# The third row tile's load moved ahead of a weight load, a copy-out shared by two engines, and four column-tiled sums put into one group

## The chip, the cores and the metric

The kernel runs on one core of a Trainium2 chip. The metric is device time in microseconds (us) of that core; a kernel's time is the median of its runs. A profile is one execution with every instruction recorded; its span, from the first to the last instruction, is some 1.7 us shorter than the time reported for the same execution (196.0 for 197.67 us before the change).

Engine names in the profile are PE (TensorE, matrix products), PEld (its weight loads), DVE (VectorE), ACT (ScalarE), POOL (GpSimd) and SP (SyncE, which issues most transfers).

## The reference, cut to what matters

The input x has 2048 rows of 512 bf16 numbers. Its layer norm feeds two branches: attention with 32 heads of 16 columns over a dilated window of 8 earlier positions, and a gated feed-forward layer 1376 wide. Both are added to x.

```python
xn = _layernorm(x, axis=-1)                       # 2048 x 512
# branch A: H = 32 heads, Dh = 16, window W = 8, dilation 2
qkv = x @ wqkv                                    # wqkv 512 x 1536: Wq, Wk, Wv
logits = einsum("bhsd,bhswd->bhsw", q, kg) * scale
attn = softmax(where(mask, logits, -1e9))
o = einsum("bhsw,bhswd->bhsd", attn, vg)          # the weighted values
# branch B
h = _gelu(xn @ w_gate) * (xn @ w_up)              # 512 x 1376 each
return x + o @ wo + h @ w_down
```

## The kernel before

The rows are worked in four blocks of 512, each of four row tiles of 128 rows. For a row tile, VectorE computes statistics, subtracts the mean and multiplies by the reciprocal of the square root; the tile is transposed, and TensorE projects it to Q, K and V and to the gate and up parts of the feed-forward layer.

The program is not written in the order in which it runs. Python code describes tasks, each with an engine, an estimated duration, what it reads and writes, and a priority; a list scheduler then fixes the order of each engine's instructions and assigns the PSUM banks. A table `SHIFT` moves the priorities of whole groups of tasks and was found by search. So a change of one part can reorder everything else.

Three places are touched by the change. First, the loads at the start. A lower number is issued earlier:

```python
# weights, 512 KB each: Wq, Wk, Wv
t_w = G.task("sp", "ld_w" + nm, 0, mk(), wr=[(I_wq, nm)],
             prio=(-958, -957.5, -898)[i], nbytes=512 * 1024)
...
if p == 0:                       # row tiles 0 and 1, 128 KB each
    for t2 in range(2):
        ...
        t_x = G.task("sp", "ld_x0_%d" % t2, 0, mk_ld(), wr=[(it_x, t2)], prio=-960 + t2,
                     nbytes=128 * 1024)
else:                            # later tiles in pairs, 256 KB
    ...
    t_x = G.task("sp", "ld_x%d" % p, 0, mk_ld(), wr=[(it_x, 0), (it_x, 1)],
                 prio=(0, -957, -897.5, -897)[p] if p < 4 else -950 + p * 20, nbytes=256 * 1024)
```

So the queue carries tile 0, tile 1, Wq, Wk, then tiles 2 and 3 together.

Second, the layer norm and the transposes of block 0. TensorE transposes a tile (four 128x128 pieces into PSUM, the memory that takes TensorE's results) and ScalarE copies all four out at once. The square roots of tiles 0 and 1 run on ScalarE (`NSQA` = 2), those of tiles 2 and 3 on GpSimd. The order of the start is fixed by chains:

```python
t_ev = G.task("act", "evx" + nm, d_act(512 * n), mk_ev(), rd=[it_tp], ...)   # one copy, 512 columns
...
chain(["bnst0", "bnag0", "sub0", "rstd0", "norm0", "bnst1", "bnag1", "sub1", "rstd1", "norm1",
       "bnst2", "bnag2", "ve2", "sub2", "bnst3", "rstd2", "norm2", "bnag3", "ve3", "sub3", "rstd3",
       "norm3", "bnst4"])
...
chain(warm_tasks[:WARM[0]] + ["tpx0_0"] + warm_tasks[WARM[0]:] +
      ["mmt0_0", "tpx0_1", "mmt1_0", "mmt0_1", "tpx1_0", "mmt1_1", "tpx1_1",
       "mmt0_2", "mmt1_2", "mmt0_3", "mmt1_3"])
```

Here `tpx0_0` to `tpx1_1` are the transposes of tiles 0 to 3, and `mmtW_T` is the projection of tile T to Q (W = 0) or K (W = 1). `warm` tasks are matrix products of zeros that run before any data is there.

Third, the sum of the weighted values. VectorE multiplies values by softmax weights into eight buffers a block; TensorE sums over partitions with a 128x32 matrix of ones, in four column tiles (`tile_position`), two of the four sums of a block in a group:

```python
pvr_grp.append((dq, it_pv, it_o))
if len(pvr_grp) == PVR_MERGE:                    # 2
    ...
    for (dq_, itp, it) in grp:
        for half in range(2):
            for d4 in range(4):
                ins = e.matmul(PS[32 * d4:32 * d4 + 32, 512 * it.slot:512 * it.slot + 512],
                               lhsT=E4[:, :], rhs=UNI[:, itp[half].slot, d4, :],
                               start=(half == 0), stop=(half == 1),
                               tile_position=(0, 32 * d4))
    ...
    # then one ScalarE copy (evo) for each sum of the group, PSUM -> OT
```

## Time and profile before

| | kernel before |
|---|---|
| time, median of 4 runs | 197.88 us (197.62 to 197.93) |
| span of the profiled run | 196.0 us |
| fourth row tile's transposes start | 12.15 us |
| last matrix product ends | 193.56 us |
| between the two ("the rest") | 181.41 us |

The busy shares, the waits of TensorE and the chain of waits are shown in the prediction below. These lines of the timeline of the kernel before give start in us, duration in us, engine, line, operation, output<-input, shape and count; in brackets stands the idle time just before, and what ended it.

```profile
6.39 1.07 PE L1076 MATMUL PS<-xnT,Wqkv 128*128 128x128 bf16 x16 [0.26 <-ACT xnT L1037]
...
7.51 1.95 PE L1076 MATMUL PS<-xnT,Wqkv 128*128 128x128 bf16 x32
...
8.13 0.69 DVE L945 BATCH_NORM_STATS2 st<-XIN 128x6 f32<-128x512 bf16 x1 [1.04 <-DMA XIN<-in_A_x_dram]
...
12.15 0.40 PE L1026 MATMUL PS<-ident,XIN 128*128 128x128 bf16 x4 [0.26 <-DVE XIN L1001]
```

The first projections (Q of tile 0) wait for ScalarE's copy. The next ones, at 7.51, are the first that need Wk, and they do not wait: Wk was there by then. The statistics of tile 2 wait 1.04 us for a transfer, because its load stands behind Wk.

### The profile page before, as it was taken

Reading aid. Unit: us, or ns where it says so; the run is one execution under the profiler, and the core shown is the slowest. Engines: PE = TensorE matmul, PEld = TensorE weight load, DVE = VectorE, ACT = ScalarE, POOL = GpSimd, SP = SyncE. Lnnn points to the kernel's source line nnn. Section 1 sums busy time; section 2 is a strip of 40 time slices with the busy share of each in tenths; the row PEclk is TensorE's granted clock in tenths of the full one; section 3 lists DMA queues with packets and bytes.
Section 4 is the critical chain, followed back from the end, with each engine's and each line's share of the span. In section 5 each row is a group of like instructions: output and inputs, shape, how many; then the busy total and the mean of one; then the engine's idle time right before and its main releaser. Section 6 shows DMA issues by size and latency. Waiting matters only on the chain.

```text
span 196.0 us, 3243 instructions
## 1 busy us (share of the span) xinstructions
PE 190.6 (97%) x1223; PEld 91.1 (46%) x1223; DVE 153.8 (79%) x241; ACT 104.0 (53%) x169; POOL 9.6 (5%) x33
## 2 busy tenths in 40 slices
PE   7879999999999999999999999999999999999995
PEld 2675444444444344444444444443444444344484
DVE  5689997999699899989989984999966638962232
ACT  3467674777976649502647801667739500776000
POOL 6021000101000000000001100000000000000000
PEclk9999999999999999999999999999999999999999
DMA  5999998949934452262399346003892250020121
GB/s 137 364 410 274 331 201 138 270 116 229 213 72 108 107 151 68 64 168 93 107 204 222 61 113 183 27 0 110 211 229 43 57 160 29 27 59 0 33 87 40
DMA packets 34783, 27.03 MB, mean 138 GB/s; under 512 B 11248, under 2 KB 33232, under 8 KB 34768
## 3 DMA queue, kind: packets, MB, share of 16 engines
q1 hardware_dynamic: 34768, 26.83, 54.0%
q8 instruction: 9, 0.15, 0.3%
q14 instruction: 6, 0.05, 0.1%
HBM read 19.99 MB, written 5.26 MB: 129 GB/s over the span
## 4 chain that ended last, share of the span: by engine, by line
PE 93%; DMA 3%; DVE 2%; SPq 1%; issue 0%; POOL 0%; DVEq 0%
PE PS L1357 36%; PE PS L1436 19%; PE PS L1120 18%; PE PS L1432 7%; PE PS L1326 4%; PE PS L1204 4%; DMA XIN<-in_A_x_dram 3%; PE PS L1076 2%; PE PS L1392 2%; PE PS L1197 1%; DVE st L945 1%; SPq L881 0%; SPq L929 0%; DVE XIN L1001 0%; POOL sq L969 0%
## 5 line engine op out<-in xcount | busy, mean ns | idle before, releaser
L1436 PE MATMUL PS<-Wd,HT 128*128 128x512 bf16 (+2 forms) x209 | 41.3, 345 | 0.0
L1357 PE MATMUL PS<-xnT,Wu 128*128 128x512 bf16 x160 | 40.6, 379 | 0.0
L1357 PE MATMUL PS<-xnT,Wg 128*128 128x512 bf16 x160 | 40.3, 379 | 0.0
L1367 ACT ACTIVATE GG<-PS 128x512 bf16<-128x512 f32 x40 | 23.7, 601 | 28.9 <-PE PS L1357 27.7
L1305 DVE TENSOR_TENSOR UNI<-BS,PT 128x2048 bf16<-128x2048 bf16 x32 | 37.1, 1217 | 2.2 <-PE PS L1326 0.8
L1174 DVE TENSOR_TENSOR UNI<-QT,KT 128x2048 bf16<-128x2048 bf16 x32 | 37.4, 1217 | 0.3 <-PE PS L1326 0.3
L1120 PE MATMUL PS<-xnT,Wqkv 128*128 128x512 bf16 x160 | 36.0, 379 | 0.0
L1374 ACT ACTIVATE UU<-PS 128x512 bf16<-128x512 f32 x40 | 24.0, 600 | 10.5 <-PE PS L1357 10.4
L1436 PEld LDWEIGHTS PS<-Wd,HT 128*128 128x128 bf16 x209 | 19.6, 98 | 18.6
L1456 DVE TENSOR_TENSOR OB<-PS,XR 128x512 bf16<-128x512 f32 (+2 forms) x19 | 11.5, 605 | 17.7 <-PE PS L1436 17.7
L1357 PEld LDWEIGHTS PS<-xnT,Wg 128*128 128x128 bf16 x160 | 15.2, 98 | 19.8 <-issue 0.8
L1357 PEld LDWEIGHTS PS<-xnT,Wu 128*128 128x128 bf16 x160 | 15.4, 98 | 19.4 <-ACT GG L1367 0.8
L1120 PEld LDWEIGHTS PS<-xnT,Wqkv 128*128 128x128 bf16 x160 | 15.4, 98 | 19.2 <-ACT KT L1137 0.4
L1379 DVE TENSOR_TENSOR HT<-GG,UU 128x512 bf16<-128x512 bf16 x40 | 16.1, 420 | 8.8 <-ACT UU L1374 8.4
L1144 ACT ACTIVATE VT<-PS 128x512 bf16<-128x512 f32 x16 | 9.6, 598 | 14.4 <-PE PS L1120 14.4
L1432 PE MATMUL PS<-Wo,OT 128*128 128x512 bf16 (+2 forms) x76 | 16.9, 345 | 0.0
L945 DVE BATCH_NORM_STATS2 st<-XIN 128x6 f32<-128x512 bf16 x16 | 10.6, 684 | 2.0 <-DMA XIN<-in_A_x_dram 2.0
L1337 ACT ACTIVATE OT<-PS 128x512 bf16<-128x512 f32 x16 | 8.7, 594 | 5.4 <-PE PS L1326 5.4
L1432 PEld LDWEIGHTS PS<-Wo,OT 128*128 128x128 bf16 x76 | 7.2, 98 | 7.0
L1137 ACT ACTIVATE KT<-PS 128x512 bf16<-128x512 f32 x12 | 7.2, 597 | 4.8 <-PE PS L1120 4.8
L1130 ACT ACTIVATE QT<-PS 128x512 bf16<-128x512 f32 x12 | 7.2, 598 | 3.8 <-PE PS L1120 3.8
L969 POOL TENSOR_TENSOR sq<-ve,mhalf 128x2 bf16<-128x2 f32 (+1 forms) x8 | 5.5, 686 | 64.3 <-DVE ve L956 64.3
(62 smaller groups left out, 134.1 us busy)
## 6 DMA issues: line engine op xcount, KB each, us to landing
BS<-vt_scratch SPq DMA_DIRECT2D x64, 128.5 KB, 3.5
vt_scratch<-VT SPq DMA_DIRECT2D x16, 128.0 KB
XR<-in_A_x_dram SPq DMA_DIRECT2D x16, 128.0 KB, 2.1
XIN<-in_A_x_dram SPq DMA_DIRECT2D x7, 256.0 KB, 5.9
out_dram<-OB SPq DMA_DIRECT2D x14, 128.0 KB, 2.0
Wqkv<-in_A_wqkv_dram SPq DMA_DIRECT2D x3, 512.0 KB, 4.3
Wg<-in_B_w_gate_dram SPq DMA_DIRECT2D x1, 1280.0 KB
Wu<-in_B_w_up_dram SPq DMA_DIRECT2D x1, 1280.0 KB
```

Of the source, the lines that this page charges most:

```text
L945: return lambda e: e.bn_stats(out=st[:, t, :], in_=XIN[:, it.slot, t2, :])
L1120: ins = e.matmul(PS[:, 512 * it.slot:512 * it.slot + HWD], lhsT=lhsT, rhs=xnT[:, itx.slot, kt, c0:c0 + HWD], start=(kt == 0), stop=(kt == 3))
L1144: return lambda e: e.activation(out=VT[:, ito.slot, 0:HWD], in_=PS[:, 512 * it.slot:512 * it.slot + HWD], func=ACTF.Identity)
L1174: return lambda e: e.tensor_tensor(out=UNI[:, it.slot, :, :], in0=bass.AP(QT, (itq.slot * 4 + g) * 512, [[NQT * 4 * 512, 128], [0, 4], [1, ...
L1305: return lambda e: e.tensor_tensor(out=bass.AP(UNI, ito.slot * 2048, [[NUNI * 2048, 128], [512, 4], [128, 4], [1, 128]]), in0=bass.AP(BS, ...
L1357: ins = e.matmul(PS[0:M, 512 * it.slot:512 * it.slot + 512], lhsT=Wx[:, kt, j * 128:j * 128 + M], rhs=xnT[:, itx.slot, kt, :], start=(kt = ...
L1367: return lambda e: e.activation(out=GG[0:M, ito.slot, :], in_=PS[0:M, 512 * it.slot:512 * it.slot + 512], func=ACTF.Gelu_apprx_tanh)
L1374: return lambda e: e.activation(out=UU[0:M, ito.slot, :], in_=PS[0:M, 512 * it.slot:512 * it.slot + 512], func=ACTF.Identity)
L1379: return lambda e: e.tensor_tensor(out=HT[0:M, ito.slot, j, :], in0=GG[0:M, ig.slot, :], in1=UU[0:M, iu.slot, :], op=ALU.mult)
L1432: ins = e.matmul(PS[:, 512 * it.slot:512 * it.slot + CW], lhsT=OT[:, ito.slot, dq, ti * 128:(ti + 1) * 128], rhs=Wo[:, dq, c0:c1], start=( ...
L1436: ins = e.matmul(PS[:, 512 * it.slot:512 * it.slot + CW], lhsT=HT[:, ith.slot, j, ti * 128:(ti + 1) * 128], rhs=Wd[:, j, c0:c1], start=Fal ...
L1456: return lambda e: e.tensor_tensor(out=OB[:, ito.slot, 0:CW], in0=PS[:, 512 * it.slot:512 * it.slot + CW], in1=XR[:, itx.slot, c0:c1], op= ...
```

## The change

It has two aims. At the start, tiles 2 and 3 are loaded apart and tile 2 comes ahead of Wk, so that its layer norm can begin while Wk is still on its way; the first copy-out is split between ScalarE and VectorE; the square roots of tiles 2 and 3 move to ScalarE. Later, all four sums of a block form one column-tiled group, so that TensorE changes its tiling mode less often. `SHIFT` and the scheduler's tolerance were searched anew. The core of the diff, with cuts marked by "...":

```diff
 SHIFT = {
-    "acc0": 47, "acc1": -436, "acc3": 127, ...
+    "acc0": -425, "acc2": -535, "acc3": 96, ...
 }
-             TOL=dict(pe=0.6, act=-0.3, dve=-0.3, pool=-0.3, sp=0.0))
+             TOL=dict(pe=0.6, act=-0.3, dve=0, pool=-0.3, sp=0.0))
...
-    NSQA = cfg.get("NSQA", 2)
+    NSQA = cfg.get("NSQA", 4)
...
-    QUOTAS = cfg.get("QUOTAS", dict(tp=2, qkv=2, lg=2, o=cfg.get("PVR_MERGE", 2), ffn=3,
+    QUOTAS = cfg.get("QUOTAS", dict(tp=2, qkv=2, lg=2, o=cfg.get("PVR_MERGE", 4), ffn=3,
...
-    PVR_MERGE = cfg.get("PVR_MERGE", 2)
+    PVR_MERGE = cfg.get("PVR_MERGE", 4)
...
-        WARM = cfg.get("WARM", (9, 1))
+        WARM = cfg.get("WARM", ([512] * 8 + [128], [512, 128]))
...
-            if p == 0:
+            if p < 2:
                 for t2 in range(2):
...
-                    t_x = G.task("sp", "ld_x0_%d" % t2, 0, mk_ld(), wr=[(it_x, t2)], prio=-960 + t2,
-                                 nbytes=128 * 1024)
+                    t_x = G.task("sp", "ld_x%d_%d" % (p, t2), 0, mk_ld(), wr=[(it_x, t2)],
+                                 prio=((-960, -959), (-957.8, -956.5))[p][t2], nbytes=128 * 1024)
...
+                if p == 0 and grp[0] == 0:
+                    def mk_ev2(it=it_t2, itx=XTI[b], o=o):
+                        return lambda e: e.tensor_copy(
+                            out=xnT[:, itx.slot, 2:4, o:o + 128],
+                            in_=PSB[:, 1024 * it.slot + 256:1024 * it.slot + 512].rearrange("q (k c) -> q k c", k=2))
+                    t_of["evy" + nm] = G.task("dve", "evy" + nm, d_dve(256), mk_ev2(), rd=[it_t2], ...)
+                nk = 2 if "evy" + nm in t_of else 4
...
-        chain(["bnst0", "bnag0", "sub0", "rstd0", "norm0", "bnst1", "bnag1", "sub1", "rstd1", "norm1",
-               "bnst2", "bnag2", "ve2", "sub2", "bnst3", "rstd2", "norm2", "bnag3", "ve3", "sub3", "rstd3",
-               "norm3", "bnst4"])
+        chain(["bnst0", "bnag0", "sub0", "rstd0", "norm0", "bnst1", "bnag1", "evy0_0", "sub1", "rstd1", "norm1",
+               "bnst2", "bnag2", "sub2", "rstd2", "norm2", "bnst3", "bnag3", "sub3", "rstd3", "norm3", "bnst4"])
...
+                chain(["evk0_0", "sq3"])
```

## The prediction

> **What bounds the kernel now.** I read three views of the profile of the kernel before, in this order: the page's busy shares (part 1), the waits of TensorE alone, then the chain that ended last in order of time. Busy shares first, to see which engine could be the bound at all:
>
> ```profile
> PE 190.6 (97%) x1223; PEld 91.1 (46%) x1223; DVE 153.8 (79%) x241; ACT 104.0 (53%) x169; POOL 9.6 (5%) x33
> ```
>
> TensorE is at 97%. A busy share can hide waits, so next all waits of TensorE, longest first (us in total, times, longest):
>
> ```profile
> PE PS L1026 <- DVE XIN L1001: 1.4, 2, 1.1
> PE PS L864 <- DVE wsrc L813: 1.2, 1, 1.2
> PE PS L1076 <- ACT xnT L1037: 0.3, 1, 0.3
> ```
>
> That is the whole list: 2.9 us, and by their lines (transposes L1026, warm-up L864, the first projections L1076) all of it is start-up. The chain (start us, us, what) shows where start-up ends and what follows:
>
> ```profile
> 2.74 5.37 DMA XIN<-in_A_x_dram
> 8.11 0.02 issue
> 8.13 0.70 DVE st L945
> ...
> 10.90 0.61 POOL sq L969
> ...
> 11.74 0.36 DVE XIN L1001
> 12.10 0.05 issue
> 12.15 0.40 PE PS L1026 x4
> 12.55 3.57 PE PS L1076 x64
> ...
> 97.23 1.84 PE PS L1204 x32
> 99.08 0.86 PE PS L1326 x16
> 99.94 5.29 PE PS L1357 x24
> 105.22 0.98 PE PS L1326 x16
> 106.20 1.83 PE PS L1357 x8
> ```
>
> Two things are to be seen. From 12.15 us, where the fourth row tile's transposes start, to 193.56 us the chain is TensorE alone: 181.4 us without a gap. Before that it is the arrival of the third and fourth row tiles (one 256 KB transfer, landed 8.11), then VectorE's layer norm of both, with a square root on GpSimd in the middle. So time can be won in two places only: before 12.15, or in the cost of TensorE's own instructions after it. After 193.56 there are an addition and a store, which the change leaves alone.
>
> **What the Trainium skill says.** TensorEngine Tiling (Array Packing), section Key Properties: "Mode switching requires drain". The trace agrees, and prices it: 16 column-tiled matmuls (L1326) take 0.98 us after ordinary ones but 0.86 right behind another column-tiled group (at 99.08), so 0.12 to enter; the 8 ordinary ones after them take 1.83 against 1.73 for 8 elsewhere in the chain, so 0.10 to leave. TensorE: Matmul & The Clock Gate, section HAM clock gate: the array starts at half clock and is released after about 3.4 us of activity, in a window that does not start with the kernel. The trace agrees: nine 512-wide warm-up matmuls take 4.02 us (0.45 each), later ones 0.216. DMA: Bandwidth & Descriptors, section Queues, rings and completion order: an engine consumes its descriptors in ring order; that is why moving an issue ahead of a 512 KB weight moves its landing. No landing of a single piece in the trace contradicts it. Perfetto Trace Analysis, section Optimizing Scalar/DVE Operations: a fixed cost per operation, so that halves cost more than half. I use it for one estimate below.
>
> **The change, part by part.**
>
> 1. Row tile order. The queue carried tiles 0 and 1 (256 KB), Wq, Wk (512 KB each), tiles 2+3 (256 KB). It will carry tiles 0, 1, Wq, tile 2, Wk, tile 3. By the stretches of the trace the transfers had moved 0.71 MB by 5.0 us, 1.10 by 6.0, 1.46 by 7.0, 1.83 by 8.0. Tiles 2+3 end at 1.57 MB, moved at 7.3, and landed at 8.11: 0.8 later. With the same lag (estimates): Wq, at 0.79 MB, lands about 6.0 in both; tile 2 at 0.92 MB: 5.5 + 0.8 = 6.3 instead of 8.1; Wk at 1.44 MB: 7.7 instead of about 7.4; tile 3 unchanged at 8.1.
>
> 2. First copy-out by two engines, and a shorter warm-up. Eight wide and one quarter-wide warm-up matmuls instead of nine wide end 0.3 us sooner, so the first transposes start when the normalised tile is there (4.79) at about 4.85, not 5.06. ScalarE's copy of 512 columns takes 0.60; I estimate 0.36 for half of it. VectorE's half fits after its second aggregate (ends 5.60) and I estimate 0.35. The first projections then start near 6.0, not 6.39, unless Wq lands later.
>
> 3. Square roots of tiles 2 and 3 on ScalarE, not GpSimd: 0.30 (L959) for 0.15 + 0.61 (L956, L969), and no hand-over through VectorE.
>
> Walk the new start, each duration from the trace of before. VectorE: tile 1 normalised at about 6.9 (7.10 before; its copy delays it 0.35, the earlier square root pays that back). Statistics 0.69, aggregate 0.18, square root 0.30, reciprocal 0.15, scale 0.35 with hand-overs: tile 2 normalised at 8.7. The order of instructions on ScalarE shows one snag: tile 1's copy-out now stands behind tile 2's square root, so it runs 8.1 to 8.7, and tile 1's Q projection can't start before 8.8 (8.4 before). It takes 0.9: 9.7; transposes of tile 2: 9.9; tile 1's K projection: 10.8. Tile 3: statistics from 8.7, after it landed, to 9.35, normalised about 10.4, in time. So the fourth transposes start near 10.8 instead of 12.15: **1.3 us saved**, on the path.
>
> 4. One column-tiled group per block for the weighted sums, not two. Matmuls stay: 128 L1326 instructions. Only mode changes go. Before: 4 groups for the logits and 8 for the sums, one of which (99.08) stands directly behind a logits group, so 11 excursions. After, by the instruction order: 4 + 4, none adjacent, so 8. Three fewer at 0.12 + 0.10: **0.66 us saved**, on the path since TensorE has no slack. Its price: all eight products of a block (8 x 1.217 us of VectorE, L1305) must be ready at once, and four PSUM banks are held until ScalarE has made four copies (4 x 0.594, L1337) where two were held.
>
> 5. New shifts: the order of the rest changes on all engines, with the same work. Nothing is saved where TensorE has no gap; gaps can only be added.
>
> Sum: 1.3 + 0.66 = 2.0 us of 197.85, so 195.9. I add 0.1 for small gaps in a reshuffled order: **196.0 us**, 0.9% less.
>
> **The rivals.**
>
> (a) A new wait in the middle takes the saving back. For it: a merged group waits for the last of eight products, VectorE is at 90% or more in about half of the slices before 160 us, four banks are held for 2.4 us, and every block has been reordered. Against it: the schedule keeps its 1.6 us margin for TensorE behind other engines, which left no wait in the kernel before; and behind each merged group except one the order has three or more matmul groups of 0.86 us, and ScalarE copies at 0.6, so it catches up. A wait of 0.3 us per block would make it 197.2; the whole 2 us would make it "no change".
>
> (b) Start-up gains only the first copy-out, because transfers bind. If tile 2 lands at 7.3 instead of 6.3, statistics start 0.4 later and all behind them: 196.4. If Wk came only at 8.5, tile 1's Q projection would wait behind K of tile 0 and slip by about 0.6: 196.6. Against both: the queue moves 340 to 385 KB per us by then, and the order of bytes is known.
>
> (c) Start-up gains more. If ScalarE's square root did not hold tile 1's copy-out (or were earlier), tile 3's normalisation at 10.4 would be the limit: 0.4 more, 195.6.
>
> (d) The gate weights bind. Wg starts near 18.0 us instead of 18.7. The bytes up to the end of Wg and Wu are moved by about 13 and 16.5 us, so this is hidden anyway; it would show as a TensorE wait on a transfer.
>
> **Range and chances.** Low: rival (c) plus a little, 195.2. High: (a) with a few tenths per block or (b), 197.2. For 2% faster the time would have to be under 193.9; more than 4 us would have to go, and no waits of that size exist: 2.9 us of TensorE waits in all, 1.2 of which come before any data. Faster 2%. For 2% slower rival (a) would need some 6 us of new waits in a schedule made to avoid them: 2%. Same: 96%.
>
> **What would show it right or wrong.** In the chain of the kernel after: the last normalisation-bound transposes near 10.8 (9.9 to 11.3 supports step 3; 12 refutes it); the VectorE statistics of tile 2 start straight behind the normalisation of tile 1 and are no longer released by the transfer. The chain from there on is TensorE alone, some 180.75 us long, ending about 191.6. Merged groups of 32 L1329 matmuls take 1.84 each, four of them. The waits of TensorE list no line beyond start-up; a wait of the merged group on VectorE products, or of a feed-forward group on a ScalarE copy, would be rival (a). The prediction would be wrong most likely through such waits, which I can't see in an instruction order without times.

## The result, and the profile after

| | before | after |
|---|---|---|
| time, median of 4 runs | 197.88 us (197.62 to 197.93) | 196.44 us (196.34 to 196.53) |
| span of the profiled run | 196.0 us | 194.8 us |
| first projections that need Wk start | 7.51 us | 8.30 us |
| fourth row tile's transposes start | 12.15 us | 11.22 us |
| last matrix product ends | 193.56 us | 192.38 us |
| the rest | 181.41 us | 181.16 us |

The ratio of after to before is 0.993, with a 95% interval of 0.9913 to 0.9947: 0.7% less time, well inside 2%. A ratio here is the mean time of one kernel's runs over that of the other's runs of the same rounds, so it is not quite the ratio of the medians quoted beside it. Executions over 1.5% slower than the fastest of the same kernel are left out of the means.

The busy shares of the kernel after (page, part 1) move little; its 1205 matrix instructions are not fewer in the program but missing in the record, since the weight loads beside them count 1224:

```profile
PE 187.7 (96%) x1205; PEld 91.3 (47%) x1224; DVE 153.3 (79%) x240; ACT 101.5 (52%) x171; POOL 16.0 (8%) x31
```

The waits of TensorE, kernel after (us in total, times, longest), the first five:

```profile
PE PS L863 <- DVE wsrc L812: 1.2, 1, 1.2
PE PS L1077 <- DVE XIN L993: 1.0, 1, 1.0
PE PS L1360 <- issue: 0.6, 4, 0.2
PE PS L1077 <- DMA Wqkv<-in_A_wqkv_dram: 0.5, 1, 0.5
PE PS L1360 <- ACT GG L1370: 0.2, 1, 0.2
```

Before, transposes waited for normalised tiles (L1026 on L1001). That wait is gone, and in its place the list has a longer wait of the first projections (1.0 us, see below) and two lines that the list of before did not have: a projection waits for a transfer of Wqkv, and a feed-forward product (L1360) waits for ScalarE. The pieces called "issue" are mostly holes left by missing records: between 36.60 and 59.98 us, for instance, the chain steps over to VectorE, but in run c below the same 108 products are in the record without a hole and take 23.42 us (36.01 to 59.43), as against 23.38 here.

The chain of the kernel after (start, us, what):

```profile
2.74 5.52 DMA Wqkv<-in_A_wqkv_dram
...
8.30 1.96 PE PS L1077 x32
...
11.61 3.57 PE PS L1077 x64
...
80.62 1.84 PE PS L1329 x32
...
150.15 0.05 issue
150.19 1.90 PE PS L1360 x8
...
191.75 0.63 PE PS L1439 x11
```

The chain's start has changed hands: the transfer of Wk to 8.26 us, where it had been the transfer of the row tiles and then VectorE and GpSimd up to 12.15. The merged groups are there, 32 matrix products in 1.84 us. At 150.15 the chain has a piece in the middle that it did not have before.

The timeline of the start, kernel after:

```profile
5.28 0.38 ACT L1039 ACTIVATE xnT<-PS 128x256 bf16<-128x256 bf16 x1 [1.12 <-PE PS L1019]
...
6.51 1.05 PE L1077 MATMUL PS<-xnT,Wqkv 128*128 128x128 bf16 x16 [0.99 <-DVE XIN L993]
...
6.78 0.69 DVE L937 BATCH_NORM_STATS2 st<-XIN 128x6 f32<-128x512 bf16 x1 [0.26 <-DMA XIN<-in_A_x_dram]
...
8.30 1.96 PE L1077 MATMUL PS<-xnT,Wqkv 128*128 128x128 bf16 x32 [0.52 <-DMA Wqkv<-in_A_wqkv_dram]
...
11.22 0.39 PE L1019 MATMUL PS<-ident,XIN 128*128 128x128 bf16 x4
```

Compare it line by line with the start of before. The statistics of tile 2 begin at 6.78 instead of 8.13: the earlier load works. The fourth transposes no longer wait for anything. But the projections that need Wk begin at 8.30 instead of 7.51, after 0.52 us of waiting for it. And the first projections begin at 6.51, though both half copies were done by 5.8 (VectorE's, 5.52 to 5.78, took 0.26). The profile names VectorE's instruction L993 as the releaser of that wait, but these products read the copied xnT and Wq, not XIN; Wq's landing is the likelier cause, which this profile does not show (in the profiles of b and d below the same wait, up to 6.24 and 6.49 us, is put down to the transfer of Wqkv).

When Wk landed can be dated in every profile, also where TensorE did not wait for it: the program lets SyncE issue the load of Wg only when Wk is complete (`t_w.deps.add(t_ld["wk"])`), and the profile shows SyncE waiting for that transfer. The issue of Wg, first in the kernel before, then in the kernel after:

```profile
7.46 0.37 SPq L890 DMA_DIRECT2D Wg<-in_B_w_gate_dram  x1
...
8.27 0.37 SPq L881 DMA_DIRECT2D Wg<-in_B_w_gate_dram  x1
```

So Wk landed at about 7.46 us before, as the prediction had it (7.4), and at 8.27 after (7.7 told).

Then the new piece in the middle. The timeline near 150 us, kernel after:

```profile
148.25 1.28 ACT L1370 ACT_TABLE_LOAD   x1
149.54 0.60 ACT L1370 ACTIVATE GG<-PS 128x512 bf16<-128x512 f32 x1
...
150.19 1.04 PE L1360 MATMUL PS<-xnT,Wu 128*128 128x512 bf16 x4 [0.24 <-ACT GG L1370]
```

ScalarE runs the exponential of block 3 (at 146.72, L1252), which needs a table load of 1.28 us before it and another behind it, to go back to the activation of the feed-forward layer. The exponential itself takes 1.01. In that time the feed-forward products that TensorE makes are not copied out of PSUM, and TensorE stops. The gaps there come to 0.42 us (found by experiment g below); which bank it waits for was not followed up.

So in the profiles: 0.93 us from the start (12.15 to 11.22), and 0.25 from the rest (181.41 to 181.16), 1.18 in all, beside 1.2 of span. The times of the two profiled executions differ by 1.14 (197.67 and 196.53), the medians by 1.44 us.

### The profile page after: what moved, and what is told of

It is laid out like the page before. It is cut to its first block, busy times and chain, and to the rows that moved or that the text cites. A ratio compares the mean times of both kernels' runs of the same rounds, so it can differ in the third digit from the quotient of the medians.

```text
span 194.8 us, 3216 instructions
## 1 busy us (share of the span) xinstructions
PE 187.7 (96%) x1205; PEld 91.3 (47%) x1224; DVE 153.3 (79%) x240; ACT 101.5 (52%) x171; POOL 16.0 (8%) x31
## 4 chain that ended last, share of the span: by engine, by line
PE 77%; DVE 15%; DMA 3%; issue 2%; ACT 2%; SPq 1%; DVEq 0%
PE PS L1360 24%; PE PS L1439 19%; PE PS L1123 12%; PE PS L1435 7%; DVE UNI L1177 5%; PE PS L1207 4%; PE PS L1329 4%; PE PS L1077 3%; DMA Wqkv<-in_A_wqkv_dram 3%; DVE UNI L1308 2%; PE PS L1395 2%; DVE HT L1382 2%; DVE PS L1245 1%; DVE ms L1240 1%; PE PS L1200 1%
## 5 line engine op out<-in xcount | busy, mean ns | idle before, releaser
L1360 PE MATMUL PS<-xnT,Wu 128*128 128x512 bf16 x157 | 39.9, 379 | 0.6 <-issue 0.3
L1360 PE MATMUL PS<-xnT,Wg 128*128 128x512 bf16 x155 | 39.3, 379 | 0.5 <-issue 0.3
L1123 PE MATMUL PS<-xnT,Wqkv 128*128 128x512 bf16 x155 | 34.9, 379 | 0.4 <-issue 0.2
L1360 PEld LDWEIGHTS PS<-xnT,Wu 128*128 128x128 bf16 x160 | 15.3, 98 | 20.0 <-issue 0.8
L1360 PEld LDWEIGHTS PS<-xnT,Wg 128*128 128x128 bf16 x160 | 15.5, 98 | 19.3 <-issue 0.8
L1163 POOL COPY KT<-KT 128x64 bf16<-128x64 bf16 x3 | 8.4, 2799 | 16.6 <-ACT KT L1140 16.6
L1077 PE MATMUL PS<-xnT,Wqkv 128*128 128x128 bf16 x128 | 7.8, 219 | 1.5 <-DVE XIN L993 1.0
```

The source lines that it names most:

```text
L1077: ins = e.matmul(PS[:, 512 * it.slot + 128 * g:512 * it.slot + 128 * g + 128], lhsT=Wqkv[:, kt, which * 512 + g * 128:which * 512 + (g + 1 ...
L1123: ins = e.matmul(PS[:, 512 * it.slot:512 * it.slot + HWD], lhsT=lhsT, rhs=xnT[:, itx.slot, kt, c0:c0 + HWD], start=(kt == 0), stop=(kt == 3))
L1360: ins = e.matmul(PS[0:M, 512 * it.slot:512 * it.slot + 512], lhsT=Wx[:, kt, j * 128:j * 128 + M], rhs=xnT[:, itx.slot, kt, :], start=(kt = ...
```

## The experiments

Eleven kernels were run, five rounds each, all with correct results. Runs a to d share one chip and its runs of the kernel before (median 197.64), f to i another (197.58), k, e and j a third (197.50).

Because any edit makes the scheduler reorder everything, all but b and k were built with a pinned order: the list of task names of each engine, taken from the kernel after (for a: from the kernel before, behind the start), and a scheduler that may place only the next name in the list. Only the named edit then differs, and in some the numbers of PSUM banks. In c, d, e and h, whose edits concern the start, the rest comes out at the 181.16 us of the kernel after.

| run | what it is | median us (range, runs) | ratio (95%) | Wk landed | Wk projections start | fourth transposes start | rest |
|---|---|---|---|---|---|---|---|
| a_start | before + start-up parts only | 196.58 (196.20–196.87, 6) | 0.9944 (0.9929–0.9959) | 8.28 | 8.31 | 11.22 | 181.41 |
| b_merge_free | before + merge only | 201.89 (201.50–203.46, 6) | 1.0236 (1.0206–1.0267) | 7.57 | 7.60 | 12.28 | 184.69 |
| c_onecopy | after, one copy-out engine | 196.13 (195.99–196.41, 6) | 0.9924 (0.9911–0.9937) | 7.72 | 7.75 | 10.66 | 181.16 |
| d_tile2late | after, tile 2 behind Wk | 197.13 (196.81–197.78, 6) | 0.9977 (0.9958–0.9996) | 7.87 | 7.90 | 12.06 | 181.16 |
| f_split | after, merged groups cut in two | 197.42 (197.22–198.38, 6) | 0.9997 (0.9981–1.0012) | 8.83 | 8.86 | 11.78 | 182.42 |
| g_logits3 | after, block 3's logits earlier | 195.66 (195.48–196.08, 4) | 0.9905 (0.9892–0.9918) | 8.24 | 8.27 | 11.18 | 180.74 |
| h_tile1act | after, tile 1's load from ScalarE | 196.37 (196.29–196.75, 5) | 0.9942 (0.9929–0.9954) | 8.09 | 8.12 | 11.03 | 181.16 |
| i_both | g and h | 195.86 (195.84–195.86, 4) | 0.9912 (0.9899–0.9924) | 7.72 | no wait | 10.96 | 180.74 |
| k_after | the kernel after again | 196.10 (195.96–196.68, 6) | 0.9927 (0.9913–0.9942) | 8.14 | 8.17 | 11.09 | 181.16 |
| e_sqpool | after, square roots on GpSimd | 196.64 (196.60–196.75, 6) | 0.9950 (0.9938–0.9962) | 7.78 | 7.81 | 11.32 | 181.16 |
| j_qfirst | g, and tile 1's Q ahead of tile 0's K | 195.60 (195.50–197.43, 6) | 0.9911 (0.9883–0.9939) | 7.93 | no wait | 10.61 | 180.74 |

The last four columns are from the one profiled run of each kernel; "Wk landed" is the issue of Wg. The last two split the time: what comes before the fourth transposes is the start, and the rest is TensorE's own chain. In the profiled executions the split is complete: the time less both parts is 4.11 to 4.19 us in twelve of the thirteen kernels (4.53 in b).

### a and b: each half of the change alone

My theory was that the start gives what the profile shows, and the merge gives its mode changes and loses part of them to a new wait. The rivals were that the start's gain is absorbed later, or that the new order and not the merge makes the difference.

Run a: the kernel after with the merge undone, and the order of before pinned behind the start.

```diff
-    PVR_MERGE = cfg.get("PVR_MERGE", 4)
+    PVR_MERGE = cfg.get("PVR_MERGE", 2)      # and the order of before
```

> The start-up part alone: the kernel before, instruction for instruction in its order from the first V projection on, with the new start-up (tile 2 between Wq and Wk, two-engine copy-out, square roots on ScalarE, shorter warm-up). Theory (start-up gains 0.93 us on the path, nothing absorbs it): the fourth transposes start near 11.2 us, the rest is TensorE alone for 181.4 us, time 196.95. Rival 1 (the gain of the start is absorbed by a later wait, e.g. on the Wg weights): 197.6 or more, with a new TensorE wait. Rival 2 (the whole 1.44 us comes from the start-up): 196.45.

The fourth transposes start at 11.22, as in the kernel after, and the rest is 181.41, to the hundredth what it was before. The median falls by 1.06 us, to 196.58. That looks nearer to rival 2's 196.45 than to the theory's 196.95, but both were counted from 197.88; from this chip's 197.64 they are 196.20 and 196.71, and the theory is the nearer. So what the start saves reaches the end undiminished; no later wait absorbs it, and no later weight load binds (its only TensorE waits are the warm-up's 1.2 us and 0.9 on Wqkv).

Run b: the kernel before with the merge alone, its own scheduler and the old shifts.

```diff
-    PVR_MERGE = cfg.get("PVR_MERGE", 2)
+    PVR_MERGE = cfg.get("PVR_MERGE", 4)
```

> The merge alone: the kernel before with one weighted-sum group per block, its old shifts, its order left to its own scheduler (the old order can't be kept: products of logits and of sums would need 16 buffers of the 12). Theory: three mode excursions fewer at 0.22 us give 197.2 if no new wait comes; every wait that comes is seen in TensorE's waits and adds to that. Rival (the new shifts are what makes the merge pay): it is not faster than before, 197.9 or more, with waits of TensorE on VectorE products or ScalarE copies that eat 0.66 us.

It is slower by 2.4%; the rival came true. The waits of TensorE in b, the longest three:

```profile
PE PS L1432 <- ACT OT L1337: 2.2, 1, 2.2
PE PS L1026 <- DVE XIN L1001: 1.4, 2, 1.2
PE PS L1357 <- ACT GG L1367: 1.3, 2, 0.7
```

One wait of 2.2 us is for ScalarE's copies of a merged group's sums, and 1.3 is for ScalarE in the feed-forward part. The rest is 184.69, which is 3.9 above the 180.75 that mode changes alone would give. The merge with its larger claim on buffers therefore does not pay in the order that the scheduler makes with the old shifts; the searched shifts and tolerance are part of the change and not decoration.

### c and d: which part of the start

The theory was that the earlier load of tile 2 is most of the start's gain; the rival was the split copy-out.

```diff
 # c: one ScalarE copy of 512 columns, as before
-                                c0 = 1024 * (it, it2)[kt // 2].slot + kt * 128 * n + q * 128
+                                c0 = 1024 * it.slot + kt * 128 * n + q * 128
-                if p == 0 and grp[0] == 0:
+                if False:
```

> The kernel after, but the first transposes copied out by ScalarE alone (one copy of 512 columns). Theory (the first projections at 6.51 us wait for the landing of Wq, so the copy is hidden): start still 6.5 us, time 196.45 within 0.1. Rival (the step of the prediction: the copy is on the path): start 0.25 later, time 196.7.

Timeline of TensorE at the start, c:

```profile
5.96 1.06 PE L1135 MATMUL PS<-xnT,Wqkv 128*128 128x128 bf16 x16 [0.43 <-ACT xnT L1097]
...
7.75 1.96 PE L1135 MATMUL PS<-xnT,Wqkv 128*128 128x128 bf16 x32 [0.51 <-DMA Wqkv<-in_A_wqkv_dram]
```

With one copy the first projections do wait 0.43 us for it, but they start at 5.96, not at the 6.5 that the theory expected, and behind them TensorE waits 0.51 us for Wk all the same. Anything won ahead of that wait is lost in it. The medians agree: 196.13 against 196.10 of the unchanged kernel (k, on another chip; ratios 0.9924 and 0.9927). The split copy-out is worth nothing that these runs can resolve (the intervals of both ratios are some 0.3 us to either side). The shorter warm-up was not undone on its own. Its profile shows something else: Wk was there at 7.75, half a microsecond earlier than in the kernel after, with the same loads in the same order.

```diff
 # d: tile 2 behind Wk again
-                                 prio=((-960, -959), (-957.8, -956.5))[p][t2], nbytes=128 * 1024)
+                                 prio=((-960, -959), (-957.2, -956.5))[p][t2], nbytes=128 * 1024)
```

> The kernel after, but tile 2 issued behind Wk instead of ahead of it (still two transfers). Theory (tile 2 ahead of Wk is what gains): VectorE's statistics of tile 2 start at 7.7 to 8.1 us instead of 6.78, the fourth transposes at 11.9 instead of 11.2, time 197.1. Rival (Wk landing later costs as much as tile 2 landing earlier gains): Wk's first projections start near 7.5 instead of 8.3 and the time stays at 196.4 or falls.

The timeline of VectorE in d shows the statistics of tile 2:

```profile
8.26 0.69 DVE L996 BATCH_NORM_STATS2 st<-XIN 128x6 f32<-128x512 bf16 x1 [1.60 <-DMA XIN<-in_A_x_dram]
```

They wait 1.60 us for the transfer (Wk landed at 7.87), and the fourth transposes start at 12.06, almost where they stood before. By the ratios d costs 0.9977 − 0.9927 = 0.005 of 197.6, about 1.0 us: nearly the whole gain of the start. The load order is the part that counts.

### e: the square roots back on GpSimd

```diff
-    NSQA = cfg.get("NSQA", 4)
+    NSQA = cfg.get("NSQA", 2)      # with ve2 and ve3 back in VectorE's chain, and without chain(["evk0_0", "sq3"])
```

> The kernel after with the square roots of tiles 2 and 3 on GpSimd again. Theory (the landing of Wk binds the start, the normalisation of tiles 2 and 3 has slack): fourth transposes at most 0.1 later, time at most 0.15 us above the kernel after. Rival (step 3 of the prediction): 0.3 us each of two tiles, 0.5 us above.

Here my expectation fell. I had come to think that, with Wk binding, the square roots were worth at most 0.15 us; the prediction's own step 3 had counted on them. The median is 196.64 against k's 196.10 on the same chip, 0.54 us more (0.45 by the ratios, whose intervals just touch). The timeline of TensorE in e:

```profile
7.81 1.96 PE L1136 MATMUL PS<-xnT,Wqkv 128*128 128x128 bf16 x32 [0.47 <-DMA Wqkv<-in_A_wqkv_dram]
...
11.32 0.40 PE L1078 MATMUL PS<-ident,XIN 128*128 128x128 bf16 x4 [0.43 <-DVE XIN L1052]
```

Wk was there at 7.81, early, and yet the fourth transposes start at 11.32: they wait 0.43 us for tile 3's normalisation, which now goes by way of GpSimd. In the runs held by Wk alone they start 2.91 or 2.92 us behind this projection (see below), which would be 10.73 here; by that the profile puts the price at 0.59. This cost and d's 1.0 overlap: together they are more than the 1.06 that the whole start gave in a. The square roots on ScalarE are what keeps this second bound out of the way whenever Wk comes early. It also fits that e's times hardly scatter (196.60 to 196.75) while k's range from 195.96 to 196.68: e would be held by its normalisation, k by the landing. That is an argument from the ranges; it was not shown run by run.

### f and g: the merged sums and the new wait

Run f cuts each merged group in two and puts two ordinary groups between the halves: four mode excursions (into the column-tiled mode and back) more, all else in order.

```diff
-                if len(pvr_grp) == PVR_MERGE:
+                if len(pvr_grp) == 2:            # first half two TensorE tasks earlier
```

> The kernel after, in its order, but each merged weighted-sum group cut in two halves with two ordinary matmul groups between them. Theory (a mode excursion costs 0.22 us of TensorE): four more excursions, 196.44 + 0.88 = 197.3; each half takes 0.98 in the chain. Rival (mode changes are hidden by something else, the merge gains by its place): 196.45.

The chain of f:

```profile
79.45 0.98 PE PS L1388 x16
80.43 1.85 PE PS L1419 x8
...
152.73 1.83 PE PS L1419 x8
154.56 0.98 PE PS L1388 x16
```

Each half costs 0.98 us and the eight ordinary products behind it 1.83 to 1.85, the prices that the prediction read from the kernel before. Four more excursions at 0.22 are 0.88; the rest grew by 1.26 (182.42 against 181.16), and the other 0.38 is put down to a longer stop of TensorE in block 3 (there the first half waits 0.73 us for ScalarE, where the kernel after has 0.24). The times agree: by the ratios f costs 0.9997 − 0.9930 = 0.0067 of 197.6, 1.3 us. Its profiled run, with the latest Wk of all (8.86), took 198.38 and is the slowest of the six; the median of 197.42 does not rest on it.

Run g leaves the merged groups whole and takes away what made TensorE stop near 150 us: the logits of block 3 are placed before an output product, so that their exponential runs 12 us earlier (at 134.69 instead of 146.72). Buffers, loads and the number of instructions stay.

```diff
 # order of TensorE:  ... acc5 acc6 acc7 er3_3 ...   ->  ... acc5 er3_3 acc6 acc7 ...
 # order of ScalarE:  exp3 moved from behind gelu3_0 to ahead of gelu2_7
 # order of VectorE:  d1_3 d2_3 ... d6_3 (softmax of block 3) and two products of block 2 moved forward with them
```

> The kernel after with the logits group of block 3 two output tiles earlier, and the exponential of block 3 (two table loads) moved with it to where ScalarE is idle. Theory (the TensorE wait near 150 us is ScalarE busy with two table loads and the exponential while feed-forward banks fill): the wait of 0.4 us on the copy out goes, 196.0. Rival (the wait moves elsewhere, or it isn't on the path): 196.4.

The chain of g around the same place:

```profile
143.06 8.58 PE PS L1419 x39
151.64 1.84 PE PS L1388 x32
```

TensorE now runs through from 143.06 into the merged group, without the pause at 150. The rest is 180.74 us; the prediction had said 180.75 for a kernel without new waits. So the price of a mode excursion was right (three fewer: 181.41 − 180.74 = 0.67), and the wait in block 3 had taken back 181.16 − 180.74 = 0.42 of it. At a ratio of 0.9905 (195.66 us), g beats both kernels.

### h and i: could Wk come earlier?

If Wk binds, an earlier issue of the queue behind tile 0 might bring it sooner. In h, ScalarE issues the load of tile 1, so that SyncE can issue Wq at 1.25 us instead of 1.72; i adds g's order.

```diff
+                    t_x.on_act = p == 0 and t2 == 1
```

> The kernel after with the load of tile 1 issued from ScalarE's queue, so that Wq, tile 2, Wk and all behind are issued 0.45 us earlier. Theory (the landings of Wq and Wk bind the start): first projections at about 6.05 instead of 6.51, K of tile 0 at 7.85 instead of 8.3, fourth transposes at 10.8, time 196.0. Rival (the transfers are limited by bytes, not by issue): no change, 196.4, or tile 0 lands later and it is slower.

> Both of the two last edits. Theory: they add, 195.55 us, 1.2% under before. Rival: they don't add, 196.0 or more.

No gain: h has 196.37, i 195.86 against g's 195.66 and the 195.55 expected. Wk landed at 8.09 in h and 7.72 in i, inside the range seen without the edit, and the statistics of tile 0 start only at 3.39 and 3.69 us instead of 2.92, so that the first transposes wait for them. Why tile 0 comes later was not followed.

### k and j: a control, and a version that doesn't need Wk early

Run k is the kernel after, unchanged, on the chip of e and j.

> The kernel after, unchanged, as the control on this chip. Every theory: ratio to before 0.993 (196.4 to 196.6 us); the TensorE-only part from the fourth transposes on is 181.16 us again, and the landing of Wk (first projection behind it) may lie anywhere between 7.7 and 8.9 us, as it did in the runs of kernels with the same loads.

In its profile the first projections start at 5.99 and Wk's at 8.17; both are earlier than in the first profile, in an identical program. Its median is 196.10, a ratio of 0.9927 as expected, though below the 196.4 told, since the kernel before is faster here too (197.50).

Run j is g with the Q projection of tile 1, which needs no Wk, ahead of the K projection of tile 0.

```diff
-                      ["mmt0_0", "tpx0_1", "mmt1_0", "mmt0_1", "tpx1_0", "mmt1_1", "tpx1_1",
+                      ["tpx0_1", "mmt0_0", "mmt0_1", "mmt1_0", "tpx1_0", "mmt1_1", "tpx1_1",
 # ScalarE: both copies of transposes and both Q copies ahead of evk0_0, and tile 1's copy ahead of sq2;
 # chain(["evk0_0", "sq3"]) dropped
```

> The version with the earlier logits group, and in the start tile 1's transposes and its Q projection ahead of tile 0's K projection. Theory (TensorE idles 0.5 to 1.6 us for Wk): the projection of Q fills that idle time, fourth transposes at 10.6 to 10.7, rest 180.75, time 195.1 to 195.2. Rival (normalisation of tile 3 takes over as the bound): fourth transposes at 11.1, time 195.6 as without it.

The timeline of TensorE in j:

```profile
6.81 2.84 PE L1136 MATMUL PS<-xnT,Wqkv 128*128 128x128 bf16 x48
...
10.61 0.39 PE L1078 MATMUL PS<-ident,XIN 128*128 128x128 bf16 x4
```

Three projections run as one piece of 48 products without a wait, the fourth transposes start at 10.61, and the rest is 180.74: the mechanism held. Two orders changed at once here, since tile 1's copy-out also stands ahead of tile 2's square root; what each is worth was not parted. The wait at the start has moved to the transposes of tile 1, which wait 1.06 us for its normalisation (6.58). The time, 195.60, did not reach the 195.1 that I expected. I had subtracted the gain from g's median, but g's timed runs were themselves better than its profiled one (that one, at 196.08, is the slowest of g's four). Counted between profiled runs it fits: that of the kernel before took 197.67; less 1.54 (12.15 to 10.61) and 0.67 gives 195.46, and j's took 195.50. One of j's six runs took 197.43, for a reason that stays open. g and j ran on different chips and can't be told apart in time.

## Why the prediction was right, and where its sizes were off

The prediction said 196.0 us, 195.2 to 197.2, and "same" at 96%; measured were 196.44 us and a ratio of 0.993. Its mechanism held for the load order, the square roots and the merge: gain at the start by the earlier tile 2, gain later by fewer mode changes, a small loss by a new wait on ScalarE. The split copy-out gave nothing. Two terms were mis-sized, and both made the gain smaller than told.

- **Step 1, the order of the loads: right that tile 2 gains, wrong by 0.6 us for Wk.** It said "Wk at 1.44 MB: 7.7"; the profile has 8.30. Tile 2 was also later than told (6.3), since its statistics at 6.78 still waited 0.26 us for it, where the prediction wanted them "no longer released by the transfer"; but this did not set the end. Wk did. In the seven profiled runs in which TensorE stands still for Wk and for nothing else behind it (after, a, c, f, g, h, k), the fourth transposes start 2.91 or 2.92 us behind the first projection that needs Wk, whether that came at 7.75 or at 8.86. So the walk's 10.8 failed in one term: had Wk come at 7.7, the same 2.92 would have given 10.6. With 8.30 it gave 11.22, and the start saved 0.93 us, not 1.3. What failed inside the step is "the same lag" of 0.8 us between bytes moved and landing: by the stretches of the traces, 1.44 MB had been moved at 7.1 us in the kernel after, 6.85 in c and 6.8 in f (estimates, as in the prediction), and Wk landed 1.2, 0.9 and 2.0 us later.
- **Rival (b) named this very path** ("tile 1's Q projection would wait behind K of tile 0"), with Wk at 8.5 and a loss of 0.6. What was argued against it, that "the order of bytes is known", is not enough: with the same loads in the same order Wk's projections started at 7.75 (c), 7.81 (e), 8.17 (k), 8.27 (g), 8.30 (after), 8.31 (a) and 8.86 us (f). One profile's landing is a sample, and a margin of a few tenths against it is none. Not the chip (7.75 and 8.31 on one) and not the issue (Wk's starts between 2.73 and 2.75 us in all seven) makes the difference; why it varies was not found. Only after and k are identical programs. Nor is all of the 0.6 us chance: with tile 2 behind it Wk landed at 7.46, 7.57 and 7.87 (before, b, d), with tile 2 ahead of it at 7.72 to 8.83, 8.15 on average of eight (these seven and j). So being passed may have cost it some 0.5 us, where 0.3 was told; but the two sets overlap, and this is read from averages.
- **Step 2, the split copy-out: durations near enough, no gain seen.** ScalarE's half took 0.38 of the whole copy's 0.60 (estimated 0.36) and VectorE's 0.26 (0.35). The first transposes did start at 4.85, as told, but they start at 4.86 in b too, with the old warm-up, so that the shorter one brings this is not shown. The prediction's escape clause, "unless Wq lands later", fits the first projections at 6.51; and even when they started at 5.96 with one copy (c), the wait for Wk swallowed the difference.
- **Step 3, the square roots: right.** Undone, they cost 0.54 us (e). The snag foreseen on ScalarE appeared as told, tile 1's copy-out behind tile 2's square root (7.92 to 8.50 us), but Wk came later still and hid it.
- **Step 4, the merge: right to a hundredth.** 0.66 us told, 0.67 measured once no wait stands beside it (g), and 0.98 and 1.84 us for groups of 16 and 32, as told.
- **Step 5 and rival (a), new gaps: 0.1 told, 0.42 measured.** The prediction argued mainly about the merged groups, where there are none; the kind that came is the other one that it named among its signs, a feed-forward group behind a ScalarE copy. It came where an exponential and its two table loads hold ScalarE while feed-forward products wait in PSUM (the stop goes when they are moved, in g; which bank was full was not followed). The instruction order without times did not tell this, as the prediction said of itself.
- **Rivals (c) and (d).** (c), more gain at the start, did not come in the kernel after but is there to be had: j, which takes tile 1's copy-out from behind the square root as (c) supposed, and puts Q ahead of K, starts its fourth transposes at 10.61. (d), the gate weights, is refuted: run a shows no such wait.

The sum by the profiles: 0.93 + 0.67 − 0.42 = 1.18 us, against 1.3 + 0.66 − 0.1 = 1.86 told. The medians show 1.44. The profiled executions bear the sum out, since their times differ by 1.14; the rest is that the profiled run of before lies 0.21 under its median and that of after 0.09 over its own. So that the time came within 0.44 us of the 196.0 is in part luck; from the profiles' 1.18 it would have been 196.70. That timed runs often had Wk earlier than the first profile fits the scatter of k, but the landing is only seen in profiled runs, so this remains an argument.

## What to carry to other kernels

When a load is moved ahead of another, walk the start a second time with the load that was passed as the late one: here the passed Wk became the bound, and the order of the products that need it decided how much of the gain was left. Take a landing time read from one profile as one sample, and where an independent product can run ahead of the one that needs the transfer, try it first (j's profile gained by it; its time can't be told from g's). Price mode changes from the trace, which was exact here, but look for the loss of a reordering where another engine is held by something indivisible, such as an exponential between two table loads.

## What the Trainium skill lacked or had wrong

- *TensorEngine Tiling (Array Packing)*, section Key Properties, says that changing the tiling mode drains TensorE and gives no price. In these runs an excursion into 32-column tiles and back cost 0.12 us to enter and 0.10 to leave, and three fewer of them shortened the rest of the kernel by 0.67 us (181.41 to 180.74).
- *DMA: Bandwidth & Descriptors*, section Latency and other measured facts, gives an HBM access latency of 0.2 us on average and 2 us at high load. What it lacks is how far the landing of one given transfer scatters from run to run: with the same loads in the same order, Wk's 512 KB landed between 7.72 and 8.83 us in eight profiled runs. No run here shows that HBM latency is the cause.
- None of the pages that I drew on tells that an exponential set between other activations can stop TensorE by way of PSUM: two table loads of 1.28 us around an exponential of 1.01 us held ScalarE for 3.6 us, and TensorE lost 0.42 us of it.
